# A fused attention and soft mixture kernel: the token weights of its last stage are turned by float32r products and spread over the projection, and its first output transfers are halved

## The chip, the cores and the metric

The kernel runs on one core of one Trainium2 chip. The metric is the device time of one execution in microseconds (us), the median of three runs. The profile comes from one further execution, taken by the hardware profiler.

## What is computed

Attention over 4 sequences of 768 tokens with 8 heads of 64, with a local window and a few global keys, and then a soft mixture of 8 experts with 4 slots each. The mixture is the part that the change touches:

```
logits = x @ phi                                  # x: 3072 x 512 (all tokens), phi: 512 x 32
d = softmax of logits over the tokens;  slot_input = d.T @ x
h = relu(slot_input[e] @ w1[e]);  slot_out[e] = h @ w2[e]   # w1: 512 x 1024, w2: 1024 x 512, per expert
c = softmax of logits over the 32 slots
return c @ slot_out                               # 3072 x 512, float32
```

## The kernel before, in words

Attention runs over 16 units (a sequence and a pair of heads each) in an order that is written out by hand (ORDER, line 56): one long list of steps for all engines, under a manual schedule, so that every engine's instructions stand in the order in which the program names them. It ends at about 155 us of the profile; the change leaves it alone. Behind it comes the mixture's tail, whose order is simply the order of the lines from 884 on:

- `softmax` (line 154) makes c for all tokens at once in the tile lnat, 120 tokens to a column block, 8 blocks to a sequence (7 of them hold tokens, the last of these 48).
- `hidden` (line 110) makes h for four experts at a time, a = 0 and a = 1, in products of 32 output columns each, four of which share the array. `hidden_t` (line 126) turns h for one a on TensorE (tile htp) and copies it out with ScalarE (ACT) and VectorE (DVE).
- `split` (line 166) writes c for one sequence in two parts: a float32r rounding (line 172, ACT) and what is left of it (line 173, DVE), so that each slot stands in four columns out of 128. Before, it is called for all four sequences while `hidden` runs on TensorE, each into a place of its own (sps, in two weight buffers whose weights were used up).
- `weights_by_slot` (line 176) turns these parts for one sequence into the tile ct, with slots on the partitions: 7 transposes on TensorE into the tile ctp (line 183; six of 120 tokens and one of 48), a copy of four of them by ACT (line 187) and of three by DVE (line 189). Before, the four sequences follow each other between `hidden_t` and the projection.
- `project` (line 141) makes h @ w2 for one half n of the 512 output columns and for one a, in eight chunks c, into one accumulator per half (the tile a). The program takes project(0, 0), project(0, 1), then project(1, 0) and project(1, 1).
- `slots_out` (line 191) turns an accumulator into sots with two DVE instructions (lines 194 and 195).
- `combine` (line 197) makes c @ slot_out for 128 tokens at a time: a product of ct with sots, two of them in one bank (tile cp, line 209), a copy of the bank by ACT (line 212) or DVE (line 214) in turn, and one transfer to the output for every group of `size` token tiles (line 215, issued by SyncE, SP). A token tile of one half is 128 x 256 numbers, 128 KB. There are 24 token tiles; six buffers (obs) of four tiles each hold what is on its way out.
- `check_inputs` (line 861) computes a flag from the inputs' ranges with 13 small DVE instructions and one transpose (tile xt, line 869); `set_flag` (line 879) writes it. A general version of the kernel would run if it were set; it isn't.

The last weights (the second half of w2's output columns) are loaded on SP's queue while this goes on; the output's transfers stand behind them in the same queue. Six banks of PSUM take turns for htp, ctp, xt, ft and cp.

Of the kernel before, what the change touches and what calls it, by code (L numbers as in the profile page):

```python
# [10 lines left out]
F32 = mybir.dt.float32  # L11
F32R = mybir.dt.float32r
# [4 lines left out]
ALU = mybir.AluOpType  # L17
# [4 lines left out]
B, H, S, D = 4, 8, 768, 64  # L22
DM = H * D
NG = 8
KB = 120
P = 128
NJ = 7
# [52 lines left out]
class Moe:  # L80


    def __init__(self, tc, ident, sgn):
        self.nc, self.ident, self.sgn = tc.nc, ident, sgn

    def constants(self):

        nc = self.nc
        low = self.ident.rearrange("p (s x m) -> p s x m", s=4, x=2)[:, :, 1, :]
        nc.vector.tensor_reduce(out=self.sgn[:, 1:2], in_=low, axis=AX.XY, op=ALU.add)  # L90
        nc.vector.tensor_scalar(out=self.sgn[:, 0:1], in0=self.sgn[:, 1:2], scalar1=-2.0, scalar2=1.0, op0=ALU.mult, op1=ALU.add)
# [74 lines left out]
    def split(self, ex, sp):  # L166

        nc = self.nc
        rows, n = ex.shape[0], ex.shape[1]
        sv = sp.rearrange("p n (s x y k) -> p (n s) x y k", s=4, x=2, y=2)  # L170
        ev = ex.rearrange("p n (s k) -> p (n s) k", k=8).unsqueeze(2).to_broadcast([rows, 4 * n, 2, 8])
        nc.scalar.copy(out=sv[:, :, :, 0].bitcast(F32R), in_=ev)
        nc.vector.tensor_tensor(out=sv[:, :, :, 1], in0=ev, in1=sv[:, :, :, 0], op=ALU.subtract)

    def weights_by_slot(self, ps, sp, ct, tiles):

        nc = self.nc
        for k in range(0, len(tiles), 4):
            part = tiles[k:k + 4]
            tp = ps.tile([P, 512], F32, name="ctp", tag="x")  # L180
            at = 0
            for i, r, t0 in part:
                nc.tensor.transpose(out=tp[:, at:at + r], in_=sp[0:r, i], identity=self.ident[0:r, 0:r])
                at += r
            c = slice(part[0][2], part[0][2] + at)
            if k % 8 == 0:
                nc.scalar.copy(out=ct[:, c], in_=tp[:, 0:at])
            else:
                nc.vector.tensor_copy(out=ct[:, c], in_=tp[:, 0:at])
# [103 lines left out]
def tile_attention_moe(ctx: ExitStack, tc: tile.TileContext, qk, v, phi, w1, w2, nn, out):  # L293
# [19 lines left out]
    flag = const.tile([P, 1], I32, name="flag")  # L313
    ngl = nv[:, 0:1]
    nlo = nv[:, 1:2]
    moe = Moe(tc, ident, sgn)

    units = [(b, p) for b in range(B) for p in range(NP)]
    nu = len(units)
# [77 lines left out]
    def load_w(pieces, c0=0, c1=WP):  # L397

        for k in pieces:
            m, e, half = piece(k)  # L400
            nc.sync.dma_start(out=places[k][:, c0:c1], in_=(w1, w2)[m][e][:, WP * half + c0:WP * half + c1])
# [450 lines left out]
    tail = ExitStack()  # L852
    ts = tail.enter_context(tc.tile_pool(name="ts", bufs=1))
    ct = ts.tile([P, B * S], F32R, name="ct")
    ohs = ts.tile([P, DM], F32R, name="ohs")
    sots = ts.tile([P, DM], F32R, name="sots")
    fl = keep.tile([P, 12], F32, name="fl")
    cst = keep.tile([KB, 8 * B, 4], F32, name="cst")
# [20 lines left out]
    def set_flag():  # L879
        ft = left.tile([P, 512], F32, name="ft", tag="x")  # L880
        nc.tensor.matmul(out=ft[0:1, 0:1], lhsT=fl[:, 9:10], rhs=ones[:, 0:1], start=True, stop=True)
        nc.vector.tensor_scalar(out=flag[0:1], in0=ft[0:1, 0:1], scalar1=0.5, scalar2=None, op0=ALU.is_ge)

    sps = [places[(5, 7)[b // 2]][0:KB, 8 * P * (b % 2):8 * P * (b % 2) + 8 * P].rearrange("p (n m) -> p n m", m=P) for b in range(B)]
    hts = [places[15][:, DF * a:DF * a + DF].rearrange("p (c m) -> p c m", c=8) for a in range(2)]
    hss = [places[6][:, DF * a:DF * a + DF] for a in range(2)]

# [2 lines left out]
    nc.vector.tensor_scalar(out=fl[0:KB, 0:1], in0=fl[0:KB, 0:1], scalar1=NEG, scalar2=None, op0=ALU.is_ge)  # L890
    moe.constants()
    moe.softmax(lnat, cst, lnat)
    for a in range(2):
        moe.hidden(left, Moe.slot_view(sl), lambda e, half: wt[0, e, half], a, hss[a])
        if a == 0:
            for b in range(B):
                moe.split(lnat[:, 8 * b:8 * b + 8], sps[b])
            for c in (0, WP // 2):
                load_w(range(npl, 28), c, c + WP // 2)
        else:  # L900
            for c in range(0, WP, WP // 4):
                load_w(range(28, 32), c, c + WP // 4)
    for a in range(2):
        moe.hidden_t(left, hss[a], hts[a])
    for b in range(B):
        moe.weights_by_slot(left, sps[b], ct, [(4 * (t % 2) + t // 2, TN[t], S * b + KB * t) for t in range(NJ)])
    check_inputs()

    obs = [places[16 + i // 2][:, 4 * HF * (i % 2):4 * HF * (i % 2) + 4 * HF] for i in range(6)]
    ops = [left.apart(n) for n in range(2)]  # L910

    def project(n, a, cs=range(8)):
        moe.project(ops[n], hts[a], lambda e, h: wt[1, e, h], n, a, cs)

    def slots_out(n):
        at, w = OUT_PART[n]
        moe.slots_out(ops[n][:, 0:w], ohs[:, at:at + w], sots[:, at:at + w])

    def combine(n, t0, sizes):
        at, w = OUT_PART[n]  # L920
        moe.combine(left, ct, n, sots[:, at:at + w], obs, out, t0, sizes)

    project(0, 0)
    project(0, 1)
    slots_out(0)
    set_flag()
    project(1, 0, range(3))
    combine(0, 0, (4,) * 5)
    project(1, 0, range(3, 8))
    project(1, 1)  # L930
    slots_out(1)
    combine(0, 20, (4,))
    combine(1, 0, (4,) * 6)
    order.close()
    tail.close()
    banks.close()
# [205 lines left out]
```

## Time and profile before

| | us |
|---|---|
| median of three runs | 211.65 (210.34 to 213.15) |
| the profiled execution, its own time | 213.26 |
| its span in the profile, first to last instruction | 211.5 |
| TensorE busy in the span | 182.5 (86%) |
| VectorE, ScalarE, GpSimd busy | 150.8, 127.6, 116.0 |
| output written | 6.29 MB in 12 transfers |

In the profile, times count from the span's start. The chain of waits goes back from the last instruction, at each step to what released it. The timeline lists instructions by engine with start, duration and count, merged where they are alike; PE is TensorE's products, PEld its weight loads, which may overlap them. The table by stretches gives each engine's busy time, TensorE's granted clock (PEclk), the DMA engines' busy share and the rate at which they moved bytes. A float32 product appears in the trace as two matmul records, a float32r product and a transpose as one.

### The profile page before, as it was taken

Reading aid. Unit: us, or ns where it says so; the run is one execution under the profiler, and the core shown is the slowest. Engines: PE = TensorE matmul, PEld = TensorE weight load, DVE = VectorE, ACT = ScalarE, POOL = GpSimd, SP = SyncE. Lnnn points to the kernel's source line nnn. Section 1 sums busy time; section 2 is a strip of 40 time slices with the busy share of each in tenths; the row PEclk is TensorE's granted clock in tenths of the full one; section 3 lists DMA queues with packets and bytes.
Section 4 is the critical chain, followed back from the end, with each engine's and each line's share of the span. In section 5 each row is a group of like instructions: output and inputs, shape, how many; then the busy total and the mean of one; then the engine's idle time right before and its main releaser. Section 6 shows DMA issues by size and latency. Waiting matters only on the chain.

```text
span 211.5 us, 6475 instructions
## 1 busy us (share of the span) xinstructions
PE 182.5 (86%) x2649; PEld 131.8 (62%) x2649; DVE 150.8 (71%) x375; ACT 127.6 (60%) x177; POOL 116.0 (55%) x141
## 2 busy tenths in 40 slices
PE   8679799986999989999999998887699999998400
PEld 2357688765787868878788876656253366576300
DVE  4889999658889878989988999296567835153600
ACT  2429899919589768979799989642403552042400
POOL 8436989785799796998889999840000000000000
PEclk9999999998899999999999999699999999999955
DMA  4769999997998976663487678998998999459892
GB/s 115 295 193 396 397 381 380 319 343 282 336 398 314 354 291 222 240 236 118 153 276 243 223 248 248 354 373 309 369 384 275 385 397 388 163 188 315 285 337 91
DMA packets 21063, 61.40 MB, mean 290 GB/s; under 512 B 2336, under 2 KB 9376, under 8 KB 19360
## 3 DMA queue, kind: packets, MB, share of 16 engines
q1 hardware_dynamic: 20880, 60.89, 79.8%
q8 instruction: 23, 0.38, 0.7%
q14 instruction: 16, 0.13, 0.2%
q10 hardware_dynamic: 144, 0.00, 0.0%
HBM read 54.59 MB, written 6.29 MB: 288 GB/s over the span
## 4 chain that ended last, share of the span: by engine, by line
PE 49%; DMA 18%; DVE 15%; POOL 9%; issue 3%; ACT 1%; DVEq 0%; POOLq 0%; SPq 0%
DMA wa<-in_v_dram 11%; PE x L602 11%; PE sc L538 9%; PE a L149 7%; PE hp L119 7%; POOL wa L586 6%; DVE wa L527 4%; PE m L631 3%; DMA wa<-in_qk_dram 3%; DVE wa L548 3%; PE m L736 2%; DMA out_dram<-wa 2%; DMA nraw<-in_n_dram 2%; POOL wa L519 2%; PE m L661 2%
## 5 line engine op out<-in xcount | busy, mean ns | idle before, releaser
L586 POOL TENSOR_TENSOR wa<-wa 128x432 f16<-128x432 f32 x91 | 98.4, 1111 | 12.3 <-ACT wa L578 8.1
L538 PE MATMUL sc<-wa 64*128 64x216 f32 (+2 forms) x448 | 49.3, 347 | 3.6 <-DVE mx L548 2.2
L602 PE MATMUL x<-wa 128*128 128x65 f16 (+1 forms) x1248 | 45.9, 196 | 3.5 <-POOL wa L586 2.0
L602 PEld LDWEIGHTS <-wa 128*128 128x128 f16 x1248 | 41.7, 99 | 9.6 <-issue 5.2
L578 ACT CAST wa<-wa 128x1296 f16<-128x1296 f32 x31 | 39.3, 1266 | 9.1 <-PE x L602 8.2
L538 PEld LDWEIGHTS sc<-wa 64*128 64x128 f32 x448 | 37.6, 190 | 10.6 <-DVE mx L548 4.1
L568 ACT ACTIVATE wa<-wa,nb 128x1296 f32<-128x1296 f32 x32 | 43.5, 1374 | 0.5
L548 DVE CUSTOM_DVE_ANT_1 wa<-sc,wa,mx 128x864 f32<-128x864 f32 x32 | 35.6, 1114 | 3.5 <-PE sc L538 1.0
L527 DVE SCALAR_TENSOR_TENSOR wa<-wa 128x896 f16<-128x896 f32 x16 | 24.3, 1519 | 5.5 <-ACT wa L522 3.1
L548 DVE CUSTOM_DVE_ANT_1 wa<-sc,wa 128x864 f32<-128x864 f32 x16 | 16.8, 1051 | 2.6 <-POOL wa L586 1.9
L636 ACT COPY wa<-m 128x480 f32<-128x480 f32 (+1 forms) x32 | 14.3, 473 | 6.7 <-PE m L631 6.7
L212 ACT COPY wa<-cp 128x512 f32<-128x512 f32 x12 | 6.3, 596 | 17.0 <-PE cp L209 15.3
L619 DVE CUSTOM_DVE_ANT_1 xn<-x,rc 120x448 f32<-120x448 f32 x24 | 14.9, 622 | 0.7
L522 ACT ACTIVATE wa<-wa 128x896 f16<-128x896 f32 x8 | 7.6, 951 | 11.4 <-DMA wa<-in_v_dram 10.5
L631 PE MATMUL m<-ident,xn 120*128 120x120 f32 x84 | 12.9, 276 | 1.1 <-DVE xmax L619 0.5
L519 POOL TENSOR_SCALAR wa<-wa 128x896 f16<-128x896 f32 x8 | 7.5, 941 | 10.7 <-DMA wa<-in_v_dram 8.4
L631 PEld LDWEIGHTS m<-ident,xn 120*128 120x128 f32 x84 | 8.6, 140 | 3.2 <-ACT wa L636 1.5
L119 PE MATMUL hp<-wp,sl 128*32 128x512 f32 x96 | 10.5, 593 | 0.0
L661 PE MATMUL m<-wa,phis 128*32 128x240 f32 (+1 forms) x128 | 9.5, 332 | 0.2 <-ACT wa L636 0.2
L214 DVE COPY wa<-cp 128x512 f32<-128x512 f32 x12 | 7.5, 682 | 2.1 <-PE cp L209 1.2
L609 DVE TENSOR_TENSOR rsall<-x,eps 120x7 f32<-120x7 f32 x32 | 5.0, 157 | 5.3 <-PE x L602 4.9
L561 PEld LDWEIGHTS m<-mm,bsel 2*128 2x128 f32 x32 | 4.7, 182 | 5.6 <-DVE mm L558 3.1
(163 smaller groups left out, 207.8 us busy)
## 6 DMA issues: line engine op xcount, KB each, us to landing
wa<-in_qk_dram SPq DMA_DIRECT2D x15, 832.0 KB, 6.6
wp<-in_w_dram SPq DMA_DIRECT2D x12, 1024.0 KB, 7.9
wa<-in_v_dram SPq DMA_DIRECT2D x16, 448.0 KB, 3.9
out_dram<-wa SPq DMA_DIRECT2D x12, 512.0 KB, 5.6
wp<-in_w_dram SPq DMA_DIRECT2D x8, 512.0 KB, 7.3
wp<-in_w_dram SPq DMA_DIRECT2D x16, 256.0 KB, 5.7
wa<-in_w_dram SPq DMA_DIRECT2D x3, 432.0 KB, 4.9
wa<-in_w_dram SPq DMA_DIRECT2D x1, 1024.0 KB, 6.8
```

The source lines that it names most:

```text
L119: nc.tensor.matmul(out=hp[n][32 * s:32 * s + 32, :], lhsT=slv(a, c, s), rhs=w1(e, c // 2)[:, (c % 2) * DF + 512 * n:(c % 2) * DF + 512 * n ...
L149: nc.tensor.matmul(out=o[32 * s:32 * s + 32, 0:w], lhsT=ht[:, c, 32 * s:32 * s + 32], rhs=w2(4 * a + s, half)[:, c0 + c * w:c0 + c * w + w ...
L527: nc.vector.scalar_tensor_tensor(out=vlo[k].rearrange(flat), in0=vraw.rearrange(flat), scalar=V_SC, in1=vhi[k].rearrange(flat)[:, :, 0:D], ...
L538: nc.tensor.matmul(out=sc[:, i, at:at + n], lhsT=r_[r, KCOL[j]:KCOL[j] + KR], rhs=r_[r, KW + KB * j:KW + KB * j + n], start=True, stop=True)
L548: nc.vector.tensor_tensor_reduce(out=tbs[u % NTB].rearrange("p (i c) -> p i c", i=2)[:, :, BW * k:BW * k + BW], in0=scs.pop((u, k))[:, :, ...
L568: nc.scalar.activation(out=head(u, i), in_=head(u, i), func=AF.Exp, bias=nbs[u], scale=T_SC)
L578: nc.scalar.copy(out=h, in_=t)
L586: (engine or nc.gpsimd).tensor_tensor(out=w, in0=t, in1=h, op=ALU.subtract)
L602: nc.tensor.matmul(out=x[:, (D + 1) * t:(D + 1) * t + d], lhsT=w[:, c:c + P], rhs=vv[:, j, i, 0:d], start=(z == 0), stop=(z == len(ops) - ...
L619: nc.vector.tensor_tensor_reduce(out=xnb[(u // 2) % 3][:, :, c:c + D], in0=out_of(u, i)[:, :, 0:D], in1=rcs.pop((u, i)).unsqueeze(2).to_br ...
L631: nc.tensor.transpose(out=m[:, at:at + KB], in_=xnb[(u // 2) % 3][:, t, P * (p % 2):P * (p % 2) + P], identity=ident[0:KB, 0:KB])
L636: nc.scalar.copy(out=xtb[u % 3][:, a:a + n], in_=ms.pop((u, k))[:, 0:n])
```

## The change

Four things are changed, all in the tail:

- The turning in `weights_by_slot` is a float32r product of the split weights with a float32r identity (ones_r, made once by GpSimd) in place of a float32 transpose. `split` writes both of its parts as float32r.
- `split` and `weights_by_slot` are spread. One small tile (sp) serves all sequences in turn, so that a split waits until the products have read the one before. Sequence 0 is turned between `hidden` and `hidden_t`, sequence 1 behind `hidden_t`, sequences 2 and 3 inside project(1, 0).
- The combining of half 0 is cut in three: token tiles 0 to 11 behind two chunks of project(1, 0), 12 to 17 behind the first chunk of project(1, 1), 18 to 23 behind slots_out(1). The first transfers of each half carry two token tiles; there are 15 transfers in all, and eight output buffers.
- `check_inputs` moves from ahead of project(0, 0) to behind the combining of tiles 12 to 17, `set_flag` to the end. ohs is half as large.

The core of the diff:

```diff
+        nc.gpsimd.tensor_copy(out=self.ones_r, in_=self.ident)
...
-        nc.vector.tensor_tensor(out=sv[:, :, :, 1], in0=ev, in1=sv[:, :, :, 0], op=ALU.subtract)
+        nc.vector.tensor_tensor(out=sv[:, :, :, 1].bitcast(F32R), in0=ev, in1=sv[:, :, :, 0], op=ALU.subtract)
...
-                nc.tensor.transpose(out=tp[:, at:at + r], in_=sp[0:r, i], identity=self.ident[0:r, 0:r])
+                nc.tensor.matmul(out=tp[:, at:at + r], lhsT=sp[0:r, i].bitcast(F32R), rhs=self.ones_r[0:r, 0:r], start=True, stop=True)
...
+    sp = ts.tile([KB, NJ, P], F32, name="sp")
...
+    def split(b):
+        moe.split(lnat[:, 8 * b:8 * b + NJ], sp)
+
+    def by_slot(b):
+        moe.weights_by_slot(left, sp, ct, [(4 * (t % 2) + t // 2, TN[t], S * b + KB * t) for t in range(NJ)])
+
     for a in range(2):
         moe.hidden(left, Moe.slot_view(sl), lambda e, half: wt[0, e, half], a, hss[a])
         if a == 0:
-            for b in range(B):
-                moe.split(lnat[:, 8 * b:8 * b + 8], sps[b])
+            split(0)
...
+    by_slot(0)
+    split(1)
     for a in range(2):
         moe.hidden_t(left, hss[a], hts[a])
-    for b in range(B):
-        moe.weights_by_slot(left, sps[b], ct, [(4 * (t % 2) + t // 2, TN[t], S * b + KB * t) for t in range(NJ)])
-    check_inputs()
+    by_slot(1)
+    split(2)
...
     project(0, 0)
     project(0, 1)
     slots_out(0)
+    project(1, 0, range(2))
+    combine(0, 0, (2, 2, 4, 4))
+    project(1, 0, range(2, 5))
+    by_slot(2)
+    split(3)
+    project(1, 0, range(5, 8))
+    by_slot(3)
+    project(1, 1, range(1))
+    combine(0, 12, (4, 2))
+    check_inputs()
+    project(1, 1, range(1, 8))
+    slots_out(1)
+    combine(0, 18, (4, 2))
     set_flag()
-    project(1, 0, range(3))
-    combine(0, 0, (4,) * 5)
-    project(1, 0, range(3, 8))
-    project(1, 1)
-    slots_out(1)
-    combine(0, 20, (4,))
-    combine(1, 0, (4,) * 6)
+    combine(1, 0, (2, 2) + (4,) * 5)
```

Line numbers in the changed kernel are one higher behind line 89. On TensorE, between the last product of `hidden` and the first of the projection, this stands before (htp is the turned h, ctp the turned weights, a_2942 the accumulator of half 0, the wp buffers those of h and of the split weights):

```order
L133 MATMUL htp<-ident,wp_89 128x128 x16
L183 MATMUL ctp<-ident,wp_88 128x120 x6
L183 MATMUL ctp<-ident,wp_88 128x48
...
L183 MATMUL ctp<-ident,wp_90 128x120 x6
L183 MATMUL ctp<-ident,wp_90 128x48
...
L869 MATMUL xt<-ident,xmax 32x120
L149 MATMUL a_2942<-wa 32x256 x64
```

and this with the change (a_2906 is the accumulator of half 0):

```order
L184 MATMUL ctp<-ones_r,sp 128x120 x6
L184 MATMUL ctp<-ones_r,sp 128x48
L134 MATMUL htp<-ident,wp_90 128x128 x16
L184 MATMUL ctp<-ones_r,sp 128x120 x6
L184 MATMUL ctp<-ones_r,sp 128x48
L150 MATMUL a_2906<-wa 32x256 x64
```

Two of the four sequences and the transpose for the flag have left this place. They stand again on TensorE inside half 1's projection, whose products (L150, accumulator a_2907) are left out between the rows:

```order
L210 MATMUL cp<-sots,ct 128x256 x12
...
L184 MATMUL ctp<-ones_r,sp 128x120 x6
L184 MATMUL ctp<-ones_r,sp 128x48
...
L210 MATMUL cp<-sots,ct 128x256 x6
L870 MATMUL xt<-ident,xmax 32x120
...
L210 MATMUL cp<-sots,ct 128x256 x6
```

Before, the projection of half 1 is interrupted once, by the 20 products of combine(0, 0, (4,) * 5); now it is interrupted four times: by the 12 products above, by sequence 2 three chunks later, by sequence 3 (the same two rows once more, not shown) after another three, and by the six products with the flag's transpose one chunk behind that. The last six follow the projection's end. On VectorE, from the first half's sots to the second's, the order is now:

```order
L196 SCALAR_TENSOR_TENSOR sots<-a_2906,sgn,ohs 128x256
L215 COPY wa<-cp 128x512 x3
L190 CAST ct<-ctp 128x288
L174 TENSOR_TENSOR sp<-lnat,sp 120x56x8
L190 CAST ct<-ctp 128x288
L215 COPY wa<-cp 128x512
L864 TENSOR_REDUCE fl<-rsall 120x1
...
L878 TENSOR_SCALAR fl<-fl 128x1
L195 TENSOR_SCALAR ohs<-a_2907,sgn 128x256
L196 SCALAR_TENSOR_TENSOR sots<-a_2907,sgn,ohs 128x256
L215 COPY wa<-cp 128x512 x2
```

Copies, the last split, the flag's instructions and the next sots are queued behind each other here; before, only the write of the flag and five copies stood between the two sots, and the flag's other instructions stood ahead of the first.

More of the change, by code (lines that the diff above doesn't have):

```diff
@@ L80, with __init__ @@
 class Moe:
-    def __init__(self, tc, ident, sgn):
-        self.nc, self.ident, self.sgn = tc.nc, ident, sgn
+    def __init__(self, tc, ident, sgn, ones_r):
+        self.nc, self.ident, self.sgn, self.ones_r = tc.nc, ident, sgn, ones_r
     def constants(self):
         nc = self.nc
+        nc.gpsimd.tensor_copy(out=self.ones_r, in_=self.ident)
         low = self.ident.rearrange("p (s x m) -> p s x m", s=4, x=2)[:, :, 1, :]
@@ L315, in tile_attention_moe @@
     nlo = nv[:, 1:2]
-    moe = Moe(tc, ident, sgn)
+    moe = Moe(tc, ident, sgn, const.tile([P, P], F32R, name="ones_r"))
     units = [(b, p) for b in range(B) for p in range(NP)]
@@ L854, in tile_attention_moe @@
     ct = ts.tile([P, B * S], F32R, name="ct")
-    ohs = ts.tile([P, DM], F32R, name="ohs")
+    ohs = ts.tile([P, HF], F32R, name="ohs")
     sots = ts.tile([P, DM], F32R, name="sots")
@@ L882, in set_flag @@
         nc.vector.tensor_scalar(out=flag[0:1], in0=ft[0:1, 0:1], scalar1=0.5, scalar2=None, op0=ALU.is_ge)
-    sps = [places[(5, 7)[b // 2]][0:KB, 8 * P * (b % 2):8 * P * (b % 2) + 8 * P].rearrange("p (n m) -> p n m", m=P) for b in range(B)]
+    sp = ts.tile([KB, NJ, P], F32, name="sp")
     hts = [places[15][:, DF * a:DF * a + DF].rearrange("p (c m) -> p c m", c=8) for a in range(2)]
@@ L902, in tile_attention_moe @@
                 load_w(range(28, 32), c, c + WP // 4)
+    by_slot(0)
+    split(1)
     for a in range(2):
         moe.hidden_t(left, hss[a], hts[a])
-    for b in range(B):
-        moe.weights_by_slot(left, sps[b], ct, [(4 * (t % 2) + t // 2, TN[t], S * b + KB * t) for t in range(NJ)])
-    check_inputs()
-    obs = [places[16 + i // 2][:, 4 * HF * (i % 2):4 * HF * (i % 2) + 4 * HF] for i in range(6)]
+    by_slot(1)
+    split(2)
+    obs = [places[16 + i // 2][:, 4 * HF * (i % 2):4 * HF * (i % 2) + 4 * HF] for i in range(8)]
     ops = [left.apart(n) for n in range(2)]
@@ L916, in slots_out @@
         at, w = OUT_PART[n]
-        moe.slots_out(ops[n][:, 0:w], ohs[:, at:at + w], sots[:, at:at + w])
+        moe.slots_out(ops[n][:, 0:w], ohs[:, 0:w], sots[:, at:at + w])
     def combine(n, t0, sizes):
```

## The prediction

> **What bounds the kernel now.** I read the table by stretches first, cut where the output flows and where it doesn't, to see what the end hangs on; then the chain of waits through the tail, the timeline at the hand-overs, and the groups.
>
> ```profile
> core 0: us, PE busy (x) PEld busy (x) DVE busy (x) ACT busy (x) POOL busy (x), PEclk, DMA share, GB/s
> 187.40:195.10 7.70, 7.15 (x114) 4.38 (x113) 2.96 (x6) 1.23 (x3) 0.00 (x0) 1.00 1.03 340
> 195.10:196.00 0.90, 0.90 (x10) 0.90 (x9) 0.69 (x2) 0.88 (x2) 0.00 (x0) 1.00 0.21 50
> 196.00:207.30 11.30, 1.75 (x14) 1.52 (x13) 3.08 (x6) 2.25 (x5) 0.00 (x0) 0.75 0.98 322
> 207.30:211.50 4.20, 0.00 (x0) 0.00 (x0) 0.00 (x0) 0.00 (x0) 0.00 (x0) 0.50 0.07 26
> ```
>
> From 187.4 us on the output flows at 340 GB/s with the DMA engines full. A token tile of one half (128 KB) takes 0.385 us at that rate. The first 20 tiles are out at 195.1, the stream is dry for 0.9, and 28 tiles follow: 10.8 us from 196.0, that is 206.8; it took until 207.3, half a microsecond was lost on the way. A fixed 4.2 us follows. So the end is the moment at which the last batch can start, plus its bytes. What sets that moment is in the chain:
>
> ```profile
> 164.85 6.01 PE hp L119 x56
> 170.86 1.90 PE htp L133 x16
> 172.75 3.67 PE ctp L183 x28
> 176.42 0.21 PE xt L869
> 176.63 8.38 PE a L149 x148
> 185.01 2.59 PE cp L209 x20
> 187.59 5.79 PE a L149 x104
> ...
> 193.41 0.49 DVE ohs L194
> ...
> 194.33 0.69 DVE wa L214
> ...
> 195.08 4.12 DMA out_dram<-wa
> ```
>
> TensorE works without a break from the end of hidden (170.86) to the second ohs (193.41), which makes half 1's sots; the transfer that ends the dry spell is issued 1.67 us behind that ohs. Half 1 is 24 tiles, 9.2 us of bytes, and none of it can leave before. An earlier start of half 0 therefore helps only as far as half 1's sots comes earlier too.
>
> **The change part by part.** I count TensorE's work from 170.86 to the second ohs, since the change only rearranges it.
>
> *The products.* The transposes of one sequence are seen in PEld, and how fast weights of 128 float32 columns load where little streams behind them (32 columns) in the last dispatch:
>
> ```profile
> 173.30 0.80 PEld L183 LDWEIGHTS ctp<-ident,wp 48*128 48x128 f32 x7 [0.15 <-issue]
> 155.42 0.52 PEld L814 LDWEIGHTS ld<-zn,sacc 128*128 128x128 f32 x4 [0.41 <-DVE sacc L747]
> 155.43 0.63 PE L814 MATMUL ld<-zn,sacc 128*128 128x32 f32 x4
> 184.94 2.46 PEld L209 LDWEIGHTS cp<-sots,ct 128*128 128x128 f32 x20 [0.41 <-issue]
> L814 PEld LDWEIGHTS ld<-zn,sacc 128*128 128x128 f32 x8 | 1.0, 190 | 0.6 <-DVE sacc L747 0.4 <-issue 0.2
> L209 PEld LDWEIGHTS cp<-sots,ct 128*128 128x128 f32 x48 | 6.0, 191 | 1.6 <-issue 0.8 <-ACT wa L212 0.7
> L183 PEld LDWEIGHTS ctp<-ident,wp 120*128 120x128 f32 (+1 forms) x28 | 3.0, 140 | 0.8 <-issue 0.6
> ```
>
> A sequence of 7 transposes takes 0.80 + 0.15 = 0.95 us; 28 of them in 3.67 give 0.13 each, of which about 0.10 is the step itself, the rest the break at the block of 48 rows. L814's loads step by (0.52 - 0.19) / 3 = 0.11. The float32r products of combine load a weight as long as L814's (191 against 190 ns, a transpose 140) and step by (2.46 - 0.19) / 19 = 0.12, with 256 columns to stream. A float32r product that turns 120 tokens has such a load and only 120 columns, so I take L814's 0.11: the load decides, not the one pass. A sequence then costs 7 x 0.01 more, four of them **+0.3**. From below, a load that hides wholly leaves the streaming: a transpose streams 120 columns in 0.10, a float32r product in half, 0.05, so a sequence takes 0.95 - 7 x 0.05 = 0.6, four of them -1.4. From above, no overlap at all is the whole duration of a product in its group, 0.29, so 7 x 0.29 = 2.0 and +4.2:
>
> ```profile
> L209 PE MATMUL cp<-sots,ct 128*128 128x256 f32 x48 | 6.6, 290 | 0.5 <-DVE sots L195 0.5
> ```
>
> *The turns.* PE leaves the projection's 32-column products for 128-column loads and comes back. Before, the projection of half 1 is interrupted once: 20 products of 0.12 are 2.4, the chain has 2.59, and the weight load stood idle for 0.41 ahead of them. A turn costs between 0.2 and 0.4; I take 0.27. Now there are four (12 products, sequence 2, sequence 3, 6 products with the flag's transpose): three more, **+0.8**.
>
> *The cover of the first sots.* Its two instructions take 1 us on DVE, and PE projects meanwhile:
>
> ```profile
> 183.54 1.46 PE L149 MATMUL a<-wp,wa 128*32 128x256 f32 x21
> 183.74 0.48 DVE L194 TENSOR_SCALAR ohs<-a,sgn 128x256 fp32r<-128x256 f32 x1 [4.85 <-PE ft L881]
> 184.26 0.48 DVE L195 SCALAR_TENSOR_TENSOR sots<-a,sgn,ohs 128x256 fp32r<-128x256 f32 x1
> 186.47 17.47 SPq L215 DMA_DIRECT2D out_dram<-wa  x12
> ```
>
> Three chunks covered it to within 0.1 us. Two chunks are 0.44 shorter (104 records in 5.79 are 13 chunks), and PE now waits so long: **+0.4**. The middle holds 18 instead of 20 products of combine: **-0.25**.
>
> *What is hidden.* The splits, a copy of ct, and the flag's first and last instruction:
>
> ```profile
> 166.09 2.18 ACT L172 CAST wp<-lnat 120x512 fp32r<-120x512 f32 x4 [1.41 <-DVE lnat L164]
> 166.74 2.50 DVE L173 TENSOR_TENSOR wp<-lnat,wp 120x512 f32<-120x512 f32 x4 [0.68 <-ACT wp L172]
> 174.16 0.56 ACT L187 CAST ct<-ctp 128x480 fp32r<-128x480 f32 x1 [0.39 <-PE ctp L183]
> 176.83 0.34 DVE L863 TENSOR_REDUCE fl<-rsall 120x1 f32<-120x192 f32 x1
> 178.74 0.15 DVE L877 TENSOR_SCALAR fl<-fl 128x1 f32<-128x1 f32 x1
> L215 SPq DMA_DIRECT2D out_dram<-wa x12: 372/1010/2187, 186.5 to 202.9; - x12
> ```
>
> Split 1 stands between turning sequence 0 and using sequence 1: a copy of 0.56 (ACT), a cast of 0.5 (2.18 us for four, now 7 blocks of 8) and 0.6 on DVE, 1.7 in all beside 1.9 us of htp; without htp it would be on the path. The copies of htp now queue behind it on both engines, and project(0, 0) waits for them no longer than for sequence 1. Split 3 is the same chain beside three chunks (1.3 us) and the rest of sequence 2; nearly hidden, at most 0.4. The flag's 13 instructions took from 176.83 to 178.9 behind the projection; now they are queued ahead of the second ohs and behind the last copy of tiles 12 to 17, about 191.6 by my sum, so done by 193.7, ahead of the ohs at 194.6. The cast of ones_r runs on a GpSimd that is idle there. The three transfers more cost SP nothing as long as one is issued (0.37 us at the shortest) in less time than its two tiles flow (0.77).
>
> *The sum.* 0.3 + 0.8 + 0.4 - 0.25: the second ohs comes **1.2 us later**, at 194.6. The front does get faster: two sequences instead of four ahead of project(0, 0), 3.9 us instead of 5.8, and a first transfer that waits for one copy less (0.4) leaves at 184.2 instead of 186.5. But its 12 tiles are out at 189.7; tiles 12 to 17 are ready about 191.6 and flow from 192.6; the stream is dry for nearly 3 us, and again for 2 ahead of tiles 18 to 23, which now stand behind the second sots. Thirty tiles then follow the second ohs where 28 did: **+0.8**. They flow from 194.6 + 1.67 + 0.94 = 197.2 for 11.55 us, to 208.8, and the span is 213.0, against 211.5 with the half microsecond lost on the way. If that loss comes again it is 213.5. I take the middle, +1.7. The profiled execution took 213.26 in all, 1.8 more than its span and 1.6 over the median; I put the difference on the median: 211.65 + 1.7 = **213.3 us**, 0.8% more. A measurement of this kernel can tell about 2% (4.2 us) from no change, so this is no change.
>
> **The rivals.**
>
> *The load hides.* If float32r loads overlap as transposes' do and the one pass sets the step (0.05), the sum loses 1.7, but sequence 3 then waits for split 3, about 0.3: 213.3 - 1.4 = 211.9. For it: transposes step at their streaming time. Against it: three groups of untransposed loads show 190 ns where transposes show 140, and L814 steps at 0.11 with 32 columns. The Trainium skill, "TensorE: Matmul & The Clock Gate", section "Back-to-back issue gap", has pairs of load and product of 128 columns at about 81 ns sustained, which lies between the two; by that figure, an estimate, four sequences would come to -0.5 instead of +0.3. No row here has such a pair in float32r.
>
> *The stream decides, not TensorE.* If what counts is when the first bytes leave and the later batches keep up with it, the whole 2.3 us at the front come through: 209.3. For it: 7.7 us at the full rate. Against it: the dry spell ahead of the second sots is there already, and the chain runs through PE.
>
> *No overlap.* If a float32r product of this shape takes its 0.29, the sum is 3.9 worse: 217.2, slower by 2.6%. It takes the time over the 2% from about 0.24 a product on. Against it: combine's products overlap.
>
> *Each transfer pays.* The shortest time from issue to landing of a transfer, 3.2 us, is 1.7 more than its bytes; three more transfers in series would add 5.0, 216.7.
>
> ```profile
> DMA to landing us min/median/max: 3.2/5.6/7.2
> ```
>
> Twelve in series would need 38 us from the first issue, 186.47, and they had landed within 23. The Trainium skill, "DMA: Bandwidth & Descriptors", section "Rules for kernel authors", asks for 1 MiB or more per transfer at full bandwidth, which speaks against smaller ones; here 512 KB ran at 340 GB/s, so I give it little.
>
> **How the numbers follow.** The forecast gets 0.55, the hidden load 0.20, the stream 0.13, no overlap 0.07, transfers in series 0.02, and 0.03 stay for what I don't see. The three runs spread over 210.3 to 213.2, so a median may be off by one. The range runs from 210.0, which leaves most of the stream's case out, to 215.2, the forecast with a split 3 that isn't hidden, turns of 0.4 and some of the noise. Faster by over 2% (under 207.4) would need more than the whole start: 0.02. Slower by over 2% (over 215.9) is no overlap and the serial transfers, with little from elsewhere: 0.08. Within 2%: 0.90.
>
> **What the new profile would show.** L184's loads at about 190 ns with steps of 0.11; a first transfer near 184.2 and a stream that runs dry twice, near 190 and near 195; the second ohs near 194.6, later than before; 30 tiles behind it. Steps of 0.05 to 0.08 would prove the first rival. A second ohs ahead of 193.4, or a stream without a dry spell, would make the forecast wrong.

## The result, and the profile after

The change makes the kernel slower by about 1%: 214.92 us median of 20 runs (212.56 to 218.05), against 211.64 (209.95 to 214.53) of 20 runs of the kernel before beside it. The prediction was 213.3 us (210.0 to 215.2), 0.8% more. The ratio to the kernel before is 1.0104, 95% interval 1.0069 to 1.0139, so 1.5 to 2.9 us; within 2%, as predicted. Ratios in this document leave out executions in which the chip was disturbed, here seven of the changed kernel's twenty, which is why the medians lie further apart than the ratio. The profiled execution took 212.56 us, with a span of 210.7 us.

That span is shorter than the 211.5 us of before, so the two traces can't be laid over each other by absolute time. The timeline shows where they part. Hidden's first products in the kernel before, then in the changed one (start, us, engine, line, operation, count):

```profile
156.92 10.51 PE L119 MATMUL hp<-wp,sl 128*32 128x512 f32 x96
```

```profile
154.14 10.51 PE L120 MATMUL hp<-wp,sl 128*32 128x512 f32 x96
```

These 96 products take as long in both, to the hundredth, but begin 2.8 us earlier in the second execution. Among the 14 profiled executions of this study its end lies anywhere from 167.1 to 172.9 us. Before and changed part between 45 and 55 us of the span, and small_first, an edit of the tail alone, parts from before there as well; all of the change but a cast of 0.7 us on GpSimd at 140 us stands in the tail. So everything below is counted from **hidden's end**, the point at which the prediction's sum starts. The chain of waits of the changed kernel from there:

```profile
168.08 1.03 PE ctp L184 x7
169.11 1.90 PE htp L134 x16
171.01 0.83 PE ctp L184 x7
171.84 7.09 PE a L150 x128
...
178.95 0.49 DVE ohs L195
...
179.47 0.49 DVE sots L196
...
180.10 1.67 PE cp L210 x12
181.77 1.43 PE a L150 x24
183.20 1.03 PE ctp L184 x7
184.23 1.43 PE a L150 x24
185.66 1.03 PE ctp L184 x7
186.69 0.57 PE a L150 x8
187.26 0.91 PE cp L210 x6
188.17 0.10 PE xt L870
188.27 3.16 PE a L150 x56
191.43 0.91 PE cp L210 x6
...
192.42 0.69 DVE wa L215
...
193.17 3.81 DMA out_dram<-wa
```

TensorE reaches project(0, 0) 3.76 us after hidden's end; it was 5.77. The first sots now stands in the chain itself: two chunks don't cover it. The second ohs starts at 191.50, 23.42 us after hidden's end (before 22.55), so 0.87 later although the front became 2.0 shorter. The time by stretches, cut where the output flows and where it doesn't (length; busy time of each engine; granted TensorE clock; DMA share; GB/s):

```profile
core 0: us, PE busy (x) PEld busy (x) DVE busy (x) ACT busy (x) POOL busy (x), PEclk, DMA share, GB/s
182.15:186.80 4.65, 4.65 (x62) 3.08 (x58) 1.75 (x4) 1.59 (x4) 0.00 (x0) 1.00 1.02 334
186.80:189.55 2.75, 2.75 (x43) 1.64 (x39) 1.90 (x7) 1.12 (x3) 0.00 (x0) 1.00 0.04 13
189.55:191.90 2.35, 2.35 (x40) 1.42 (x33) 1.34 (x10) 0.00 (x0) 0.00 (x0) 1.00 0.99 327
191.90:194.00 2.10, 1.90 (x16) 1.62 (x15) 2.06 (x6) 1.38 (x3) 0.00 (x0) 1.00 0.07 20
194.00:205.80 11.80, 2.10 (x16) 1.84 (x15) 3.44 (x6) 2.48 (x5) 0.00 (x0) 0.70 1.01 330
205.80:210.70 4.90, 0.00 (x0) 0.00 (x0) 0.00 (x0) 0.00 (x0) 0.00 (x0) 0.50 0.08 29
```

The stream starts 2.5 us earlier against hidden's end (the first transfer is issued at 181.23, 13.15 after it; before 15.61), and stands still for 2.75 and 2.1 us: the whole lead is given back. Thirty tiles follow from 194.0 on. Behind them the last stretch is 4.9 us, where it was 4.2.

From hidden's end to the end of the span (the **tail**) it was 40.6 us and is 42.6: +2.0, about what the ratio says (1.0104 is 2.2 us). The last transfer lands 39.5 us after hidden's end instead of 38.2.

### The profile page after: what moved, and what is told of

Same layout as the page of the kernel before. It is cut to its first block, busy times and chain, and to the rows that moved or that the text cites. A ratio compares the mean times of both kernels' runs of the same rounds, so it can differ in the third digit from the quotient of the medians.

```text
span 210.7 us, 6482 instructions
## 1 busy us (share of the span) xinstructions
PE 180.9 (86%) x2649; PEld 130.1 (62%) x2649; DVE 150.4 (71%) x375; ACT 127.5 (61%) x177; POOL 117.0 (56%) x142
## 4 chain that ended last, share of the span: by engine, by line
PE 45%; DMA 16%; DVE 16%; POOL 9%; issue 4%; ACT 3%; DVEq 0%; POOLq 0%; ACTq 0%; SPq 0%
DMA wa<-in_v_dram 12%; PE x L603 9%; PE sc L539 8%; POOL wa L587 7%; PE hp L120 7%; PE a L150 6%; DVE wa L549 4%; DVE wa L528 4%; PE m L632 3%; POOL wa L520 2%; DMA nraw<-in_n_dram 2%; DVE wa L587 2%; PE ctp L184 2%; DMA out_dram<-wa 2%; PE m L662 2%
## 5 line engine op out<-in xcount | busy, mean ns | idle before, releaser
L587 POOL TENSOR_TENSOR wa<-wa 128x432 f16<-128x432 f32 x91 | 99.7, 1126 | 8.5 <-ACT wa L579 5.5
L539 PE MATMUL sc<-wa 64*128 64x216 f32 (+2 forms) x448 | 48.1, 342 | 2.8 <-DVE mx L549 1.7
L603 PE MATMUL x<-wa 128*128 128x65 f16 (+1 forms) x1248 | 44.5, 193 | 3.7 <-POOL wa L587 2.3
L603 PEld LDWEIGHTS <-wa 128*128 128x128 f16 x1248 | 40.3, 97 | 9.9 <-issue 5.1
L579 ACT CAST wa<-wa 128x1296 f16<-128x1296 f32 x31 | 39.2, 1265 | 7.5 <-PE x L603 7.1
L539 PEld LDWEIGHTS sc<-wa 64*128 64x128 f32 x448 | 36.8, 186 | 9.5 <-issue 3.8
L528 DVE SCALAR_TENSOR_TENSOR wa<-wa 128x896 f16<-128x896 f32 x16 | 23.7, 1482 | 3.4 <-POOL wa L520 2.6
L556 PE MATMUL m<-ident,mx 128*1 128x128 f32 x32 | 6.1, 271 | 2.7 <-DVE mx L549 2.1
L150 PE MATMUL a<-wp,wa 128*32 128x256 f32 x128 | 7.9, 382 | 0.0
```

The lines of the kernel that those rows point to most:

```text
L150: nc.tensor.matmul(out=o[32 * s:32 * s + 32, 0:w], lhsT=ht[:, c, 32 * s:32 * s + 32], rhs=w2(4 * a + s, half)[:, c0 + c * w:c0 + c * w + w ...
L528: nc.vector.scalar_tensor_tensor(out=vlo[k].rearrange(flat), in0=vraw.rearrange(flat), scalar=V_SC, in1=vhi[k].rearrange(flat)[:, :, 0:D], ...
L539: nc.tensor.matmul(out=sc[:, i, at:at + n], lhsT=r_[r, KCOL[j]:KCOL[j] + KR], rhs=r_[r, KW + KB * j:KW + KB * j + n], start=True, stop=True)
L579: nc.scalar.copy(out=h, in_=t)
L587: (engine or nc.gpsimd).tensor_tensor(out=w, in0=t, in1=h, op=ALU.subtract)
L603: nc.tensor.matmul(out=x[:, (D + 1) * t:(D + 1) * t + d], lhsT=w[:, c:c + P], rhs=vv[:, j, i, 0:d], start=(z == 0), stop=(z == len(ops) - ...
```

## The experiments

All are told in the same measures, from each kernel's own profiled execution: us from hidden's end to the second ohs, to the issue of the next transfer behind it, to the last landing (the trace's records of issues and completions) and to the end; and the tiles that still had to flow at that issue. The rest column is the last landing less the issue less 0.385 us for each such tile. The ratio is to the kernel before, with its 95% interval.

| kernel | 2nd ohs | next transfer | tiles behind | last landing | rest | end | ratio |
|---|---|---|---|---|---|---|---|
| before | 22.55 | 24.22 | 28 | 38.2 | 3.2 | 40.6 | 1 |
| changed | 23.42 | 25.09 | 30 | 39.5 | 2.9 | 42.6 | 1.010 (1.007 to 1.014) |
| transposes_back | 23.19 | 24.86 | 30 | 39.8 | 3.4 | 43.2 | 1.004 (0.998 to 1.010) |
| all_tiles_between | 24.14 | 26.47 | 24 | 39.2 | 3.4 | 41.3 | 1.006 (1.000 to 1.011) |
| before_all_tiles | 23.12 | 25.78 | 24 | 38.3 | 3.3 | 40.6 | 0.995 (0.989 to 1.000) |
| small_first | 22.56 | 24.22 | 28 | 38.1 | 3.1 | 40.8 | 1.000 (0.994 to 1.005) |
| late_start | 22.70 | 24.37 | 30 | 38.8 | 2.9 | 41.9 | 1.005 (0.999 to 1.011) |
| fewer_turns | 22.96 | 24.63 | 30 | 39.3 | 3.1 | 42.6 | 1.010 (1.000 to 1.020) |
| four_repairs | 22.78 | 24.45 | 28 | 38.2 | 3.0 | 41.2 | 1.003 (0.994 to 1.012) |
| two_behind | 22.80 | 24.58 | 26 | 37.9 | 3.3 | 40.9 | 1.000 (0.994 to 1.006) |
| checks_last | 22.31 | 23.97 | 28 | 37.2 | 2.4 | 41.0 | 1.013 (1.009 to 1.017) |
| best | 22.55 | 23.60 | 26 | 36.8 | 3.2 | 41.4 | 1.014 (1.008 to 1.021) |
| large_transfers | 23.42 | 25.08 | 30 | 39.6 | 3.0 | 42.4 | 1.009 (1.004 to 1.014) |
| early_flag | 22.80 | 23.85 | 26 | 38.0 | 4.1 | 40.6 | 0.993 (0.987 to 0.998) |

Each row's positions come from one execution. The intervals of most ratios are wider than the steps that they would have to tell apart; the argument rests on the positions.

The theory: the end is the second ohs, which TensorE's unbroken work sets, plus the time until a transfer can leave, plus the bytes still behind it. Its rivals: the products themselves cost it all; the number and size of the transfers; the time of the first transfer.

### The products

```
-  nc.tensor.matmul(out=tp[:, at:at + r], lhsT=sp[0:r, i].bitcast(F32R), rhs=self.ones_r[0:r, 0:r], ...)
+  nc.tensor.transpose(out=tp[:, at:at + r], in_=sp[0:r, i], identity=self.ident[0:r, 0:r])
```

> The changed kernel with float32 transposes in place of the one-pass products; order, turns and transfers stay. The measure with the least noise is the tail, from hidden's last product to the end of the span: 40.6 us before, 42.6 with the change. Theory (TensorE's unbroken work up to the second sots, plus the bytes behind it, set the end; a float32r product steps by its weight load, 0.11 us, a transpose by 0.10): a sequence of seven goes from 1.03 to 0.95 us, the tail from 42.6 to 42.3, the time against before from 1.010 to about 1.009. Rival A (the products cost what the change costs): the tail is back at 40.6, the ratio at 1.000. Rival B (the one pass is a gain that other parts eat): a sequence takes longer than 1.03, the tail is 43 or more, the ratio over 1.013.

The groups of weight loads (busy us, mean ns of one), in the changed kernel and in this one:

```profile
L184 PEld LDWEIGHTS ctp<-ones_r,sp 120*128 120x128 f32 (+1 forms) x28 | 3.7, 190 | 1.9 <-issue 1.2 <-DVE sp L174 0.4
```

```profile
L184 PEld LDWEIGHTS ctp<-ident,sp 120*128 120x128 f32 (+1 forms) x28 | 3.0, 140 | 2.3 <-issue 1.0 <-PE hp L120 0.8 <-DVE sp L174 0.4
```

and the first two sequences in the chain with transposes:

```profile
169.97 0.96 PE ctp L184 x7
170.93 1.90 PE htp L134 x16
172.82 0.81 PE ctp L184 x7
```

A load is 190 ns against 140, and the four sequences take 1.03, 0.83, 1.03 and 1.03 us against 0.96, 0.81, 0.95 and 0.97: the second ohs comes 0.23 sooner with transposes. So the product is neither the whole cost (rival A) nor a gain (rival B, whose sign on the sequences is refuted). The tail of 43.2 that rival B asked for arose behind the ohs: 0.5 more in the rest column, and 3.4 instead of 3.1 us from the last landing to the end. The time can't tell 0.1% here. In this shape the float32r product is worth nothing; it costs 0.01 us a product. That its longer load is the reason is not shown. The transposes of h load in 141 ns,

```profile
L134 PEld LDWEIGHTS htp<-ident,wp 128*128 128x128 f32 x16 | 1.7, 141 | 0.0
```

and 16 of them take 1.90 us in the changed kernel's chain, 0.119 each, as much as the float32r products in the sequence that follows them (0.83 / 7).

### Where half 0's tiles stand

```
 all_tiles_between (of the changed kernel)     before_all_tiles (of the kernel before)
-    combine(0, 12, (4, 2))                    -    combine(0, 0, (4,) * 5)
+    combine(0, 12, (4, 4, 4))                 +    combine(0, 0, (4,) * 6)
-    combine(0, 18, (4, 2))                    -    combine(0, 20, (4,))
```

> The changed kernel with all 24 tiles of half 0 ahead of the second sots: tiles 12 to 23 go out in three transfers of 4, and none stays for behind the sots. Theory: six more products of combine ahead of the second ohs make it 0.7 us later (24.1 us after hidden's end instead of 23.4), 24 tiles instead of 30 flow behind it, 2.3 us less; the tail goes from 42.6 to 41.0, the time against before from 1.010 to about 1.003. The second dry spell of the output stream shrinks from 2 us to under 1. Rival (the order of the tiles does not matter, since the number and size of the transfers or a fixed cost behind each decide): tail 42.6, ratio 1.010. Rival (ohs queues on DVE behind the copies and the flag): ohs later than 24.6 after hidden's end, tail 41.5 or more.

> The kernel before with all 24 tiles of half 0 ahead of the second sots (20 stood there, 4 behind). Theory: four more products make the second ohs 0.5 us later (23.05 us after hidden's end instead of 22.55), 24 instead of 28 tiles flow behind it, 1.5 us less; the tail goes from 40.6 to 39.6 and the ratio to 0.995. Rival (only the time of the first transfer and the sum of the bytes count): tail 40.6, ratio 1.000. Rival (only TensorE's end counts, whatever the bytes behind it): tail 41.1, ratio 1.002.

The second ohs came where it was expected, 24.14 and 23.12. In the changed kernel the tail fell by 1.3 to 41.3 (1.6 expected), in the kernel before not at all: 40.6, where 39.6 was expected. Even the 1.3 are not what was meant: the last landing came only 0.4 sooner (39.2), and the stretch behind it took 2.1 us instead of 3.1. The chain of before_all_tiles shows the step that both expectations had missed:

```profile
194.71 0.50 DVE ohs L194
...
195.24 0.49 DVE sots L195
...
195.87 1.93 PE cp L209 x14
```

With no tile of half 0 left, nothing can be turned into PSUM while ohs and sots are made, and the next transfer leaves 2.66 us behind ohs instead of 1.67 (2.33 in all_tiles_between). In the kernel before, four tiles kept back cost 1.5 us of bytes; they spare half a microsecond of TensorE ahead of the second ohs and this microsecond behind it: nearly even. The ratio is a little more favourable than the tail (its interval ends at 1.000).

### The size of the transfers

```
 small_first (of the kernel before)            large_transfers (of the changed kernel)
-    combine(0, 0, (4,) * 5)                   -    combine(0, 0, (2, 2, 4, 4))
+    combine(0, 0, (2, 2) + (4,) * 4)          +    combine(0, 0, (4, 4, 4))
-    combine(1, 0, (4,) * 6)                   -    combine(1, 0, (2, 2) + (4,) * 5)
+    combine(1, 0, (2, 2) + (4,) * 5)          +    combine(1, 0, (4,) * 6)
```

> The kernel before with the first transfer of each half cut in two (2 and 2 tiles instead of 4, 14 transfers instead of 12) and eight buffers instead of six for them, nothing else. Theory: bytes and TensorE's order are the same; the first transfer of half 1 waits for one copy less and leaves 0.4 us sooner, that of half 0 too, but the latter gains nothing; tail 40.2 to 40.6, ratio 0.998 to 1.000. Rival (each transfer pays about 1.7 us that its bytes do not need): two more make 3.4, tail 44, ratio 1.016. Rival (smaller transfers flow slower): the first 4 tiles of each half take longer than 0.385 us a tile, tail over 41.

> The changed kernel with its first twelve tiles in three transfers of 4 and half 1 in six of 4, so 13 transfers in all instead of 15; TensorE's order and everything else stays. The runs so far show that behind the last landing SyncE still has a list of closing waits to go through: 2.4 us from its first instruction after the branch to the end in the kernel before (12 transfers), 3.1 with the change (15), 3.0 in the kernel before with 14, the difference being one pause of about 1.1 us in the list. Theory C (the number of transfers, so the length of SyncE's program, sets that pause): the last landing stays at 39.4 to 39.6 us after hidden's end, the closing stretch shrinks to 2.4 to 2.6, the tail goes from 42.6 to 42.0. Rival (the pause comes with the execution, not with the number of transfers): closing stretch 2.8 to 3.4 and tail 42.4 or more. If smaller transfers paid for themselves by an earlier start, the tail would be over 43.

Last landings of 38.1 (before 38.2) and 39.6 (changed 39.5): the sizes make no difference to the landing either way, and the rival of transfers in series is refuted. The Trainium skill, "DMA: Bandwidth & Descriptors", section "Rules for kernel authors", wants 1 MiB or more per transfer for full bandwidth; here two transfers of 256 KB and two of 512 KB flowed at 334 GB/s (182.15 to 186.80 above). The forecast of theory C fell: with 13 transfers the closing stretch, from SyncE's first instruction behind its branch to the end, was 3.2 us, no shorter than with 15.

Its idea, that the length of SyncE's program sets the pause, holds all the same. In the closing list of 21 instructions the pause stands ahead of the 14th in all four kernels with 15 transfers, ahead of the 16th in the four with 14 and an early flag, the 18th in the two with 13 and the 20th in the two with 12 and an early flag. Each transfer adds two instructions ahead of the list, so that is always the 218th of SyncE's records in the trace (in checks_last and best, which write the flag last, the 217th). With 15 transfers it lasts 1.1 to 1.4 us, with 14 1.0 to 1.2 (0.4 in all_tiles_between, where SyncE had just waited 1.2 us in the list for the last landing), with 13 0.7 and 1.0. SyncE then waits another 0.4 us for GpSimd's last steps. With 12 the pause is 0.7 us and runs while GpSimd does these steps, so that this wait is gone. The closing stretch is 3.1 to 3.4 us with 15 transfers and 2.4 and 2.5 with 12. What SyncE does in the pause the trace doesn't show.

### What TensorE turns and waits for

All three are edits of the changed kernel; late_start first:

```
-    project(1, 0, range(2))
+    project(1, 0, range(5))
     combine(0, 0, (2, 2, 4, 4))
-    project(1, 0, range(2, 5))
     by_slot(2)
```

fewer_turns:

```
     combine(0, 0, (2, 2, 4, 4))
-    project(1, 0, range(2, 5))
     by_slot(2)
     split(3)
-    project(1, 0, range(5, 8))
-    by_slot(3)
+    project(1, 0, range(2, 8))
     project(1, 1, range(1))
+    by_slot(3)
     combine(0, 12, (4, 2))
```

four_repairs is fewer_turns with these besides:

```
-    project(1, 0, range(2))
+    project(1, 0, range(3))
-    project(1, 0, range(2, 8))
+    project(1, 0, range(3, 8))
-    combine(0, 12, (4, 2))
+    combine(0, 12, (4, 4))
-    combine(0, 18, (4, 2))
+    combine(0, 20, (4,))
```

> The changed kernel with its first twelve tiles combined three chunks of projection later, directly ahead of sequence 2: the first transfer is given up 1 us of its lead, one turn of TensorE falls away, and the first sots is covered by five chunks instead of two. Theory (TensorE's work up to the second sots decides, the early start of the stream does not): the first transfer leaves 14.1 us after hidden's end instead of 13.15; the second ohs comes 0.6 us earlier (0.36 of waiting for sots and 0.27 of a turn), 22.8 instead of 23.4 us after hidden's end; the tail goes from 42.6 to 42.0. Rival (when the first bytes leave decides): the tail goes to 43.6.

> The changed kernel with sequence 2 directly behind the first twelve tiles' products and sequence 3 directly ahead of the next six: TensorE leaves the projection twice instead of four times; products, sizes and the two chunks of cover stay. Theory: two turns of 0.27 us fall away, the second ohs comes 22.9 instead of 23.4 us after hidden's end, the tail goes from 42.6 to 42.1, the time by 0.25% down. Rival (a turn is free, what TensorE lost is in the products alone): ohs at 23.4, tail 42.6.

> The changed kernel with one-pass products, two sequences ahead of the projection and the smaller transfers kept, but three chunks of cover for the first sots, two turns less, and 20 instead of 18 tiles of half 0 ahead of the second sots. Theory: this takes back 0.36, 0.54 and 0.77 us and gives 0.25 for two more products; the second ohs comes 22.8 us after hidden's end (before: 22.55, with the change 23.4), 28 tiles stand behind it as before; tail 40.8 to 41.2, ratio to before 1.001 to 1.003. Rival (the loss lies in the products, in the smaller transfers or in the place of the new tiles, which all stay): ratio still 1.010, tail 42.6.

late_start gave its first transfer up for 0.9 us (14.04 us after hidden's end instead of 13.15) and has its second ohs 0.72 earlier; the last landing came 0.7 earlier, the tail 0.7 (41.9). If the first bytes decided, it would have been later: that rival is refuted. fewer_turns moved ohs by 0.46, so a turn is 0.23 us:

```profile
180.06 1.67 PE cp L210 x12
181.74 0.83 PE ctp L184 x7
182.57 3.16 PE a L150 x56
185.73 1.03 PE ctp L184 x7
```

Directly behind combine's products the sequence takes 0.83 us, where it took 1.03 among the projection. The landing followed by 0.2 only, and the tail not (42.6): SyncE took 1.92 us to issue the second transfer behind ohs (1.54 in the changed kernel), so that half 1's first one left at 27.21 us after hidden's end, hardly ahead of 27.28. Why it took longer stays open. four_repairs keeps the products, the two sequences ahead of the projection and the small transfers, and has ohs at 22.78 and its last landing at 38.2: back at the kernel before but for 0.6 us of tail, all of it behind the last landing, where its 14 transfers put the pause. Its ratio is 1.003, but the interval (0.994 to 1.012) holds the rival's 1.010 too; the positions refute the rival. From fewer_turns to it the cover is 22.96 + 0.24 - 22.78 = 0.42 us.

### Attempts at a version that beats both

All four are edits of the kernel before; two_behind, best, early_flag and, above, small_first also have eight output buffers instead of six. two_behind:

```
-    combine(0, 0, (4,) * 5)
+    combine(0, 0, (4,) * 5 + (2,))
-    combine(0, 20, (4,))
-    combine(1, 0, (4,) * 6)
+    combine(0, 22, (2,))
+    combine(1, 0, (2, 2) + (4,) * 5)
```

checks_last moves check_inputs() and set_flag(), in this order, behind combine(1, 0, (4,) * 6). best is checks_last with

```
     combine(0, 0, (4,) * 5)
+    combine(0, 22, (2,))
-    combine(0, 20, (4,))
-    combine(1, 0, (4,) * 6)
+    combine(0, 20, (2,))
+    combine(1, 0, (2, 2) + (4,) * 5)
```

and early_flag has of this only what is said of tiles 20 to 23: the check and the flag stay early, half 1 goes out in six transfers of 4.

> The kernel before with 22 tiles of half 0 ahead of the second sots, 2 behind it (20 and 4 before), and half 1's first transfer cut in two. The run with all 24 ahead showed that the stream then resumes a microsecond later behind the second ohs, as no tile of half 0 is left whose products can run while sots is made. Theory: two tiles are enough for that; the second ohs is 0.25 us later (22.8 us after hidden's end), the two tiles leave 1.3 instead of 1.67 us behind it, 26 instead of 28 tiles flow then: tail 39.7 instead of 40.6, ratio 0.996. Rival (what is moved ahead of the sots is given back behind it in every case): tail 40.6, ratio 1.000.

> The kernel before with the input check and the flag moved behind all of combine, nothing else: the check's transpose (0.21 us in the chain) and the flag's product leave TensorE's path, the 13 VectorE instructions run while the last bytes flow. Theory: the second ohs comes 22.3 us after hidden's end instead of 22.55, the last landing 0.25 us sooner (37.9 instead of 38.2 after hidden's end), the time 0.1% down, too little to measure. Rival (the flag, read at the very end, becomes the last thing): the flag is written later than the last landing and the stretch behind the last landing, 2.5 us before, grows.

> The kernel before with the check and the flag behind all of combine, 22 tiles of half 0 ahead of the second sots and, behind it, tiles 20 and 21, whose copy is ScalarE's (22 and 23, in the run with two tiles behind, were copied by VectorE, behind ohs and sots), and half 1's first transfer cut in two. Theory (the last landing is the second ohs, plus the time until the next transfer can leave, plus 0.385 us for each tile behind it, plus 3.2): ohs 22.4 us after hidden's end, the two tiles leave 1.1 us behind it, half 1's first two 2.3 to 2.6 us behind it; last landing 37.0 to 37.5 us after hidden's end (before 38.2, with the change 39.5), ratio 0.995 to 0.997. Rival (who copies the last two tiles does not matter): they leave 1.8 us behind ohs as with VectorE; last landing 37.6 or later, ratio 0.998 or more.

> The kernel before with 22 tiles of half 0 ahead of the second sots and tiles 20 and 21, which ScalarE copies, behind it; the check and the flag stay early, half 1 stays in six transfers of 4 (13 in all). In the run with the flag last all engines reach their branch within 0.1 us of each other and SyncE's first instruction behind its branch came 4.9 us later, against 3.6 to 4.5 elsewhere, 1.1 us behind the last landing. Theory: with the flag early this is 3.5 to 4.0 us again and SyncE goes on within 0.2 us of the last landing; ohs 22.8 us after hidden's end, the two tiles leave 1.1 us behind it, last landing 37.6 to 38.0 (before 38.2), tail 40.1 to 40.6, ratio 0.997 to 1.000. Rival (the late branch is the matter of that one execution): SyncE is as late here.

two_behind landed 0.3 us earlier instead of 0.9: its two tiles left 1.8 us behind ohs, not 1.3, because VectorE copies them, behind ohs and sots. In best and early_flag, where ScalarE does, they left 1.05 us behind it. In early_flag ScalarE copies while VectorE makes sots (first the chain, then the row of sots in the timeline):

```profile
194.83 0.44 PE cp L209 x2
...
195.34 0.59 ACT wa L212
```

```profile
195.42 0.48 DVE L195 SCALAR_TENSOR_TENSOR sots<-a,sgn,ohs 128x256 fp32r<-128x256 f32 x1
```

But half 1's first transfer followed 1.66 us later, the two tiles are 0.77 us of bytes, and the stream was dry again (47 GB/s from 198.0 to 198.5); the last landing is 38.0, hardly earlier than before. In best half 1's first transfer is halved and followed after 1.28 us, and the rest column is 3.2 instead of 4.1; but the flag differs too, so what the halving is worth there stays open. early_flag's ratio, 0.993 (0.987 to 0.998), is the best measured; but it rests on five runs, its tail is that of before, and the median of its twelve runs (212.24) lies above that of the 23 of before beside it (211.85). I do not call it faster.

checks_last and best brought the last landing forward by 1.0 and 1.4 us (0.25 and 0.7 to 1.2 were expected; checks_last's rest column is the lowest of all, and why stays open), and ended later all the same (41.0 and 41.4). The flag is written here behind the last copy (timeline of checks_last):

```profile
195.57 0.69 DVE L214 COPY wa<-cp 128x512 f32<-128x512 f32 x1 [1.22 <-DMA out_dram<-wa]
...
198.60 0.15 DVE L882 TENSOR_SCALAR flag<-ft 1x1 int32<-1x1 f32 x1 [0.37 <-PE ft L881]
```

All engines read it and branch on it. By the trace's records GpSimd, TensorE, ScalarE and VectorE branched within 0.2 us of each other here, SyncE 0.2 (best: 1.1) later, and SyncE's next instruction came 4.9 us behind its branch, 1.1 us behind the last landing in both. In early_flag it was 3.4 us, ahead of the landing, so its rival is refuted, and in the eleven others 3.5 to 4.5. So the late flag has eaten the gain: SyncE came to its closing list 38.2 and 38.0 us after hidden's end, as against 38.2 before. The list then took 2.8 and 3.4 us instead of 2.4, with a pause of 1.1 and 1.5 us in it (the 217th record in both). Of checks_last's rival one half holds: the stretch behind the last landing grew from 2.4 to 3.9 us. The flag itself was written long before that landing (31.7 against 37.2 us after hidden's end). That the instructions behind the branch are fetched, and that the engines' fetches are in each other's way, is argued and was not tried. The ratios of the two, 1.013 and 1.014, are also more than these tails explain (0.4 and 0.8 us); they rest on three and four runs, and that part stays open.

## Why the prediction was right

**The anchor.** The sum was to be laid on 170.86; this execution's hidden ended at 168.08. Counted from there the steps can be compared. Taken at its word, the prediction's own sign of being wrong came true: the second ohs stood at 191.50, ahead of 193.4. Counted from hidden's end it came 0.87 us later, as the mechanism asks; to name a sign in absolute time was a mistake.

**The front.** 3.9 us to project(0, 0) were predicted, it took 3.76; the first transfer at 13.3 us after hidden's end, it left at 13.15; dry spells of nearly 3 and of 2, they were 2.75 and 2.1.

**The products, +0.3.** They cost 0.23. The load of 190 ns was right, and so was the step: by the starts of the products in the trace 0.11 us between blocks of 120 tokens, a transpose's 0.10. With the block of 48 tokens a sequence directly behind other 128-column loads takes 0.83 / 7 = 0.119 us a product, with transposes 0.81 / 7 = 0.116. The rivals of a hidden load (0.05) and of no overlap (0.29) are both refuted. The reason that the prediction gave, that the load decides, is not shown (see transposes_back). How long a float32r product streams no run isolates: combine's, with 256 columns at a step of 0.12 us, leave at most 0.056 for 120 columns, close to the 0.05 that the prediction took. The Trainium skill, "TensorE: Matmul & The Clock Gate", section "Back-to-back issue gap", has about 81 ns for a pair of a load and a product of 128 columns; in float32r it was not reached.

**The turns, +0.8.** 3 x 0.23 = 0.7. **The cover, +0.4.** 0.42 by the runs; the wait in TensorE's row is 0.36:

```profile
180.10 1.67 PE L210 MATMUL cp<-sots,ct 128*128 128x256 f32 x12 [0.36 <-DVE sots L196]
```

**Two fewer products, -0.25.** They step by 0.12, as before. Not counted was the check's transpose, 0.21 us in the chain of before and 0.10 here. Together 0.23 + 0.7 + 0.42 - 0.25 - 0.1 = 1.0; the second ohs moved by 0.87, predicted **+1.2**. The products and the turns were each put about a tenth of a microsecond too high, the check's transpose was missing, and no term had the wrong sign.

**What is hidden.** Split 1 and split 3 cost nothing that shows: the loads of the last sequence wait 0.41 us for split 3, where the turn alone has 0.41, and the sequence takes the same 1.03:

```profile
183.13 0.99 PEld L184 LDWEIGHTS ctp<-ones_r,sp 120*128 120x128 f32 x7 [0.41 <-issue]
185.59 0.99 PEld L184 LDWEIGHTS ctp<-ones_r,sp 120*128 120x128 f32 x7 [0.41 <-DVE sp L174]
190.48 0.15 DVE L878 TENSOR_SCALAR fl<-fl 128x1 f32<-128x1 f32 x1
```

The flag's instructions were over at 190.63, ahead of the ohs at 191.50.

**Thirty tiles, +0.8.** 0.77 by the rate. The last landing moved by 1.37: 0.87 + 0.77, less 0.27 in the rest column, about what the sum took off for the half microsecond lost before, which it counted by half (-0.25).

**The fixed 4.2 us.** This is the step that failed. Behind the last landing 2.4 us passed before and 3.1 with the change. It was taken as a constant, and the three added transfers were put at nothing for SyncE; among the 14 executions the stretch runs from 2.1 to 4.6 us. What changed is the pause in SyncE's closing list (see large_transfers): the three transfers make SyncE's program six instructions longer, and so the pause moves from the list's last steps, where GpSimd's work runs beside it, to a place where nothing does. The four kernels with 15 transfers take 3.0 to 3.4 us behind the last landing, the two with 12 and an early flag 2.3 and 2.4. So the 0.6 belong to the program and not to the one execution, as far as six profiles show; they are profiled executions all, and whether the pause is as long when nothing is recorded no run shows. The times speak for it: 1.37 us alone would be a ratio of 1.0065, just below the interval.

So +1.7 was forecast and +2.0 came, 1.4 of it as worked out and 0.6 from where nothing was expected, while the ohs was 0.3 less late than the sum had it; that these two partly make up for each other is luck. Of the rivals, the hidden load, the stream that decides, no overlap and the transfers in series are all excluded by runs.

## What to carry to other kernels

Where a second batch of results waits for one engine's unbroken work, an earlier start of the first batch was worth nothing here: count that engine's work up to the last producer, and the bytes still behind it. Work that moves out of the front into the middle is paid again with each turn and each cover that it breaks. And lay two traces over each other at an instruction just ahead of the change, since single executions here lay up to 5.8 us apart by then.

## What the runs showed of the hardware

The end of a kernel that branches on a flag is not only its last byte. SyncE issues the last transfer (32.1 us after hidden's end in the kernel before, 32.8 with the change), reads the flag in 0.8 to 1.2 us, branches, and has its next instruction 3.4 to 4.9 us later: at 38.2 and 39.5 us, within 0.1 us of the last landing in both. A stream that ended 1.1 us sooner than that, as in checks_last and best, gained nothing by it. In these two, with the flag written so late that all engines branch within 0.2 us (SyncE in best 1.1 later), SyncE's next instruction came 4.9 us behind its branch, in the twelve others 3.4 to 4.5.

Behind that, SyncE pauses once, at the same place of its instruction stream whatever the kernel does: ahead of the 218th of its records in all twelve kernels with an early flag, for 0.4 to 1.4 us. Three transfers more moved the closing list against this place and made the end 0.6 us longer.

A turn of TensorE from 32-column to 128-column loads and back costs 0.23 us, twice the step of a product.
